# Attention then routed MLP on one core: q of eleven units loaded twice and transposed on VectorE, with their k and v laid nine tokens to a partition

## The chip, the cores and the metric

The kernel runs on one core of one Trainium2 chip. The metric is the device time in microseconds (us) of one execution; several executions are timed and the median is quoted. A separate profile shows one execution of the same program, instruction by instruction. Names used below: PE is the matrix engine (TensorE), ACT is ScalarE, DVE is VectorE, POOL is GpSimd, SP is SyncE, whose queue issues nearly all of the plain DMAs. SBUF is the on-chip memory of 128 partitions, PSUM the accumulators that PE writes.

## The reference

The computation is an attention without a score matrix, followed by a small MLP that only 128 tokens of each batch go through. All data are float32.

```python
# q, k, v: (8 batches, 8 heads, 576 tokens, 64)
q_s = exp(q - max over d) / sum over d            # softmax over the 64 dims
k_s = exp(k - max over tokens) / sum over tokens  # softmax over the 576 tokens
kv  = einsum('bhsd,bhse->bhde', k_s, v)           # 64 x 64 for each head
x   = einsum('bhsd,bhde->bhse', q_s, kv)          # then laid out as (8, 576, 512)
...
scores = x @ w_gate                               # (8, 576)
top = the 128 tokens of the batch with the highest score
out = x; out[top] = x[top] + sigmoid(scores[top]) * (relu(x[top] @ w1) @ w2)
```

w1 is 512 x 1024, w2 is 1024 x 512.

## The kernel before

The attention is cut into 16 units: a unit `u` is four heads of one batch, and two units make a batch. For each unit the kernel loads q, k and v (L115 to L147), takes exponentials on ACT (`k_exp` L266, `q_exp` L271), copies v beside a column of ones (`v_copy` L278), multiplies k by v on PE (`kv_mm` L290), normalises that on DVE (`kv_out` L314), transposes q's exponentials on PE with the identity and copies them from PSUM to SBUF (`q_t` L328), multiplies them by the normalised product (`x_mm` L358), normalises and stores (`x_sums`, `x_scale`, `x_store`, L381 to L408). The softmax sums come out of the same products, through the columns of ones. Inside a unit the heads have the number 2i + a.

Layout. 576 tokens are 64 partitions of nine tokens (T = 9). In units 0 and 1 (`FLAT`, L103) a load puts nine tokens of a head on each of 64 partitions, a = 0 on the lower half of the partitions and a = 1 on the upper half; `kv_mm` then works with 64 x 64 quarters of PE's array (L303 to L306: nine rows by four quarters). In units 2 to 15 k and v are paired: the nine tokens are split five and four over two neighbouring partitions (`R` = 5, `N2` = 4, L138 to L143: two DMAs each for k and v), and `kv_mm` uses all 128 rows (L307 to L311: two banks by five rows by two column halves). q is always nine tokens to a partition and comes in two DMAs of five and four rows (L132 to L137). In `x_mm` every one of the 36 small products takes 64 tokens as stationary operand, `qT[part(i), a, r, c]`, where r and c name the row of the nine.

There are three buffers of q, k and v each (`raw`, LD = 3, L105), so a unit's load has to wait until the exponential three units earlier has read the buffer.

Then for each batch: `score` and `score_row` make the row of scores on all partitions, `compare` counts on DVE for each token how many are higher (L441 to L447, five instructions of 576 elements for a batch), `hits` and `find` turn the ranks into 128 row numbers, `fetch` gathers those rows of the output from DRAM on POOL (L483), `turn` transposes them on PE (L519), `mlp1` and `mlp2` are the two dense products (L535 to L555), and `finish` scatters the result (L563).

Order. The tile scheduler is off (L150); each engine runs its instructions in the order in which they are written, and so does SP's queue of DMAs. The main part is the loop of L746. Step s handles unit s: at its head `find` and `fetch` of an earlier batch when s is even, then `q_t(s)` in two halves (L835, L836), `kv_mm(s + 1)`, `x_mm(s)`, the sums, in odd steps `score` of the batch just completed, then the stores and loads (`queues`, L762: the store of unit s, then k and v of unit s + 3, then its q, the first one held until the last product of `x_mm(s)`), `q_exp(s + 1)`, in odd steps `score_row` and the five `compare`, then `k_exp(s + 2)`, `v_copy(s + 2)` and `hits`. Pieces of the dense products of the batch that is three steps back are spread between these as `pieces(...)`. Steps below 3 are written out above the loop, and step 3 is the branch of L785. In even steps the last pieces are followed by `turn` of the batch whose rows `fetch` has brought.

The x products use two pairs of PSUM banks, which `q_t` uses too; the k by v product and the row of scores share one pair of banks called kv.

Of the kernel before, what the change touches and what calls it, by code (L numbers as in the profile page):

```python
# [17 lines left out]
def kernel(  # L18
# [64 lines left out]
    def pair(tag, bufs=1):  # L83
        return ps.tile([P, 2, 512], F32, tag=tag, name=tag, bufs=bufs)
# [16 lines left out]

    LD = 3
    FLAT = 0, 1  # L103
    RR = 4 * R
    raw = {w: [const.tile([P, 2 * T if w == "q" else RR, D], F32, name=f"{w}{n}") for n in range(LD)] for w in "qkv"}  # L105

    def view(t, paired):
        return t.rearrange("p (h r) d -> p h r d", h=4) if paired else t[:, :2 * T].rearrange("p (i r) d -> p i r d", i=2)
# [6 lines left out]
    def load(u, which, after=None, split=False, flat=False):  # L115
        b, qd = units[u]
        for what in which:
            src = {"q": q, "k": k, "v": v}[what]
            first = src[place(b), 4 * qd].offset
            dmas = []  # L120
            if flat:
                t = view(raw[what][u % LD], False)
                if split:
                    for h, queue in enumerate((nc.scalar, nc.sync)):
                        dmas.append(queue.dma_start(out=t[:, h].rearrange("p r d -> p (r d)"),
                                                    in_=bass.AP(tensor=src.tensor, offset=first + 2 * h * SD,
                                                                ap=[[T * D, P], [1, T * D]])))
                else:
                    dmas.append(nc.sync.dma_start(out=t.rearrange("p i r d -> p i (r d)"),  # L129
                                                  in_=bass.AP(tensor=src.tensor, offset=first,  # L130
                                                              ap=[[T * D, P], [2 * SD, 2], [1, T * D]])))
            elif what == "q":  # L132
                t = view(raw[what][u % LD], False)
                for r0, r1 in ROWS:
                    dmas.append(nc.sync.dma_start(out=t[:, :, r0:r1].rearrange("p i r d -> p i (r d)"),  # L135
                                                  in_=bass.AP(tensor=src.tensor, offset=first + r0 * D,
                                                              ap=[[T * D, P], [2 * SD, 2], [1, (r1 - r0) * D]])))  # L137
            else:  # L138
                t = view(raw[what][u % LD], True)
                for n, rows in ((1, N2), (0, R)):  # L140
                    dmas.append(nc.sync.dma_start(out=t[n::2, :, :rows].rearrange("p h r d -> p h (r d)"),  # L141
                                                  in_=bass.AP(tensor=src.tensor, offset=first + n * R * D,
                                                              ap=[[T * D, 64], [SD, 4], [1, rows * D]])))  # L143
            if after is not None:
                behind(dmas[0], after)
                after = None
        return dmas[-1]  # L147

    ROWS = (0, R), (R, T)
    ctx.enter_context(tc.manual_schedule())  # L150
    load(0, "k", split=True, flat=True)
    load(0, "vq", flat=True)
# [27 lines left out]
    ones_b = const.tile([P, 4 * P], BF16, name="ones_b")  # L180
    nc.vector.memset(ones_b, 1.0)
    w_ps = bank("mm", 2)
    ones_f = const.tile([P, 4 * P], F32, name="ones_f")
    nc.gpsimd.memset(ones_f, 1.0)
    for n in range(WARM):
        nc.tensor.matmul(out=w_ps, lhsT=ones_f[:, :P], rhs=ones_f, start=True, stop=True)
# [20 lines left out]
    for n in range(2):  # L207
        t = const.tile([P, RR, D + 1], F32, name=f"v_ones{n}")
        nc.vector.memset(t[:, :, D:], 1.0)
        v_ones.append(t)  # L210
        t = const.tile([P, 2, C], F32, name=f"kv_w{n}")
        nc.vector.memset(t[:, :, D:D + 1], 1.0)
        kv_w.append(t)
    qrec = const.tile([P, NU, 2, G], F32, name="qrec")
    krec = const.tile([P, NU, 2], F32, name="krec")


    order_minus_p = const.tile([P, RP], F32, name="order_minus_p")
    nc.gpsimd.iota(order_minus_p, pattern=[[1, RP]], base=0, channel_multiplier=-1,
                   allow_small_or_imprecise_dtypes=True)  # L220

# [39 lines left out]
    st = {}  # L261

    def heads(t, u):
        return t[:, :2 * T].rearrange("p (r i) d -> p i r d", i=2) if u in FLAT else view(t, True)

    def k_exp(u):  # L266
        ke = heads(at.tile([P, RR, D], F32, tag="ke", name="ke"), u)
        nc.scalar.activation(out=ke, in_=view(raw["k"][u % LD], u not in FLAT), func=AF.Exp)  # L268
        st["ke", u] = ke

    def q_exp(u, c):  # L271
        if c == 0:
            st["qe", u] = at.tile([P, T, 2, D], F32, tag="qe", name="qe")
        r0, r1 = ROWS[c]
        qr = raw["q"][u % LD].rearrange("p (i r) d -> p r i d", i=2)
        nc.scalar.activation(out=st["qe", u][:, r0:r1], in_=qr[:, r0:r1], func=AF.Exp)  # L276

    def v_copy(u, engine=nc.scalar):  # L278
        out_v, in_v = heads(v_ones[u % 2], u)[:, :, :, :D], view(raw["v"][u % LD], u not in FLAT)
        if engine is nc.scalar:  # L280
            engine.copy(out=out_v, in_=in_v)  # L281
        else:
            engine.tensor_copy(out=out_v, in_=in_v)
# [6 lines left out]
    def kv_mm(u, crossed=False):  # L290

        ke, vo = st.pop(("ke", u)), heads(v_ones[u % 2], u)
        kv_ps = pair("kv")
        if crossed:
            n = 2 * (D + 1)
            for r in range(T):
                for a in range(2):
                    nc.tensor.matmul(out=kv_ps[:, a, :n], lhsT=ke[part(a), :, r],
                                     rhs=vo[part(a), :, r],
                                     start=(r == 0), stop=(r == T - 1))  # L300
            st["kv", u] = [(part(i), kv_ps[part(i), :, i * (D + 1):(i + 1) * (D + 1)]) for i in range(2)]
            return
        for r in range(T if u in FLAT else 0):  # L303
            for i, a in QUARTERS:
                nc.tensor.matmul(out=kv_ps[part(i), a, :D + 1], lhsT=ke[part(a), i, r], rhs=vo[part(a), i, r],
                                 start=(r == 0), stop=(r == T - 1))  # L306
        for a in range(0 if u in FLAT else 2):  # L307
            for r in range(R):
                for i in range(2):
                    nc.tensor.matmul(out=kv_ps[part(i), a, :D + 1], lhsT=ke[:, 2 * i + a, r], rhs=vo[:, 2 * i + a, r],  # L310
                                     start=(r == 0), stop=(r == N2))  # L311
        st["kv", u] = [(slice(0, P), kv_ps[:, :, :D + 1])]

    def kv_out(u):  # L314
# [7 lines left out]
        nc.vector.tensor_mul(prod, kw[:, :, :D], wg[:, qd])  # L322
        nc.vector.reduce_sum(out=kw[:, :, D + 1], in_=prod, axis=AX.X)


    copies = []

# [30 lines left out]
    def x_mm(u, a, wide=False, tag="x"):  # L358

        qT = st["qT", u] if a == 0 else st.pop(("qT", u))  # L360
        x = pair(tag, 2 if tag == "x" else 1)
        kw = kv_w[u % 2]
        for r in range(R):
            for i, c in QUARTERS:
                to = x[part(c), i, r * C:(r + 1) * C]
                if r == N2 and c:
                    last = nc.tensor.matmul(out=to, lhsT=ones_b[part(i), :D], rhs=ones_b[part(i), :C], start=True, stop=True)
                    continue
                if wide and r < N2:
                    if c == 0:  # L370
                        nc.tensor.matmul(out=x[:, i, r * C:(r + 1) * C],
                                         lhsT=qT[part(i), a, r].rearrange("p c t -> p (c t)"), rhs=kw[part(i), a],
                                         start=True, stop=True)
                    continue
                nc.tensor.matmul(out=to, lhsT=qT[part(i), a, r, c], rhs=kw[part(i), a], start=True, stop=True)  # L375
        st["x", u, a] = x[:, :, :R * C].rearrange("p i (r c) -> p i r c", r=R)
        return last

# [113 lines left out]
    def select(b, n, r):  # L492

        k0, m = slots[n]
        if r == 0:
            st["select", n] = bank("mm", 2), md.tile([P, R, P], F32, tag="hit_f", name="hit_f", bufs=1)
        t_ps, hit = st["select", n]
        far = md.tile([P, P], F32, tag="far", name="far")
        nc.scalar.activation(out=far[:, :m], in_=slot_no[:, k0:k0 + m], func=AF.Abs, scale=-1.0,
                             bias=st["rank", b][:, r:r + 1])  # L500
        nc.scalar.activation(out=hit[:, r, :m], in_=far[:, :m], func=AF.Relu, scale=-1.0, bias=1.0)
# [244 lines left out]
    for s in range(LAG, NU + LAG):  # L746
# [83 lines left out]
        else:  # L830
            if chosen is not None and s not in AFTER:
                pieces(1 if here else 2)
                search()
            if here:
                q_t(s, 0)  # L835
                q_t(s, 1, on_vector=s > LAG + 1)  # L836
            if follows:
                kv_mm(s + 1)
                kv_out(s + 1)
# [21 lines left out]
            pieces(0, to=2 if follows else 3)  # L861
            if ends is not None:
                rows()
                ranks()
            if s + 2 < NU:
                k_exp(s + 2)
            pieces(0, to=4)
# [4 lines left out]
                number = count_good(good)  # L872
            if ends is not None:
                each(hits, ends)
            pieces(0, to=KF - 1)
            if second and mlp_b + 1 < B:
                each(turn, mlp_b + 1)
# [35 lines left out]
```

## Time and profile before

| what | value |
|---|---|
| median of 3 timed runs | 209.97 us (209.13 to 210.23) |
| the profiled execution, its own time | 210.15 us |
| its span in the trace | 208.4 us |
| granted clock of PE, mean | 0.988 |
| PE busy | 193.6 us (93%) |
| DVE busy | 119.0 us (57%) |
| ACT busy | 92.1 us (44%) |
| POOL busy | 32.4 us (16%) |
| moved by DMA | 46.66 MB, mean 224 GB/s |

The time of a run stands 1.75 us above the span: the span begins with the first instruction of the core and ends with the last. A busy share is time in which an engine had at least one instruction in it; the chain that ended last, which the profile follows back from the end, tells which of the busy engines the end waited for. The DMA list of the page gives for each kind of load its size and the median time from issue to landing.

### The profile page before, as it was taken

The numbers are of one execution on the slowest core, as the hardware profiler recorded it, in microseconds if no ns is written. First come the engines' busy times: TensorE is split into PE (matmuls) and PEld (weight loads), VectorE is DVE, ScalarE is ACT, GpSimd is POOL, SyncE is SP. The second block draws the span as 40 slices with busy tenths as digits, with TensorE's granted clock in tenths as the row PEclk, the third lists the DMA queues.
The fourth block names the chain that finished last, engine by engine and source line by source line (L and its number), as shares of the span: only waits on it lengthen the run. The fifth ranks groups of instructions, "written<-read, shape, count | busy, mean of one in ns | idle before, by whom it ended". The sixth has DMA issues, their size and how long they took to land.

```text
span 208.4 us, 6943 instructions
## 1 busy us (share of the span) xinstructions
PE 193.6 (93%) x2955; PEld 148.8 (71%) x2955; DVE 119.0 (57%) x361; ACT 92.1 (44%) x135; POOL 32.4 (16%) x93
## 2 busy tenths in 40 slices
PE   7899799798989999999999999999999999999960
PEld 3486789785579848985698759974898579659520
DVE  6668735597167645776378717862776537714010
ACT  3468876574526624545434813672464022111100
POOL 5103000202010101210120104010211012126010
PEclk9999999999999999999999999999999999999995
DMA  6999999999786999995989779895880433131101
GB/s 218 397 307 330 384 360 372 371 381 329 193 296 158 309 327 250 283 279 170 233 282 253 231 175 304 212 314 129 256 247 4 103 110 74 48 101 53 58 5 53
DMA packets 37720, 46.66 MB, mean 224 GB/s; under 512 B 2353, under 2 KB 33073, under 8 KB 37682
## 3 DMA queue, kind: packets, MB, share of 16 engines
q1 hardware_dynamic: 36256, 41.66, 65.2%
q0 software_dynamic: 1280, 4.20, 5.7%
q8 instruction: 25, 0.41, 0.8%
q10 hardware_dynamic: 146, 0.30, 0.5%
q14 instruction: 13, 0.11, 0.2%
HBM read 34.61 MB, written 11.53 MB: 221 GB/s over the span
## 4 chain that ended last, share of the span: by engine, by line
PE 74%; DMA 16%; SPq 3%; issue 1%; ACT 1%; DVE 1%; POOL 0%; POOLq 0%; ACTq 0%
PE mm L544 25%; PE mm L554 25%; DMA k<-in_k_dram 15%; PE x L375 8%; PE kv L310 8%; PE x L349 4%; DMA xr<-out_dram,idx 2%; SPq L141 2%; PE kv L432 2%; PE mm L524 2%; SPq L135 1%; ACT ke L268 1%; PE mm L473 1%; SPq L169 0%; SPq L129 0%
## 5 line engine op out<-in xcount | busy, mean ns | idle before, releaser
L544 PE MATMUL mm<-xT,w 128*128 128x128 f32 x512 | 62.0, 278 | 0.3 <-DVE xT L532 0.3
L544 PEld LDWEIGHTS mm<-xT,w 128*128 128x128 f32 x512 | 58.8, 192 | 2.0 <-ACT xT L532 0.6
L554 PE MATMUL mm<-w,hT 128*128 128x512 f32 x128 | 59.3, 599 | 0.0
L446 DVE SCALAR_TENSOR_TENSOR junk<-srow,s,not_before 128x576 bf16<-128x576 f32 x40 | 32.7, 819 | 9.4 <-ACT srow L438 8.1
L554 PEld LDWEIGHTS mm<-w,hT 128*128 128x128 f32 x128 | 22.6, 190 | 20.6 <-issue 20.1
L567 DVE SCALAR_TENSOR_TENSOR o<-mm,g,xr 128x512 f32<-128x512 f32 x7 | 5.3, 751 | 35.6 <-PE mm L554 35.6
L395 DVE TENSOR_TENSOR xs<-x,qrec 128x640 f32<-128x640 f32 x31 | 24.1, 815 | 0.0
L375 PE MATMUL x<-kv_w,qT 64*64 64x66 f32 x1084 | 21.9, 222 | 1.7 <-issue 1.5
L268 ACT ACTIVATE ke<-k 128x1280 f32<-128x1280 f32 (+1 forms) x16 | 20.0, 1253 | 4.6 <-DMA k<-in_k_dram 4.6
L276 ACT ACTIVATE qe<-q 128x640 f32<-128x640 f32 (+1 forms) x32 | 20.1, 676 | 3.3 <-DMA q<-in_q_dram 3.3
L375 PEld LDWEIGHTS x<-kv_w,qT 64*64 64x64 f32 x1084 | 19.4, 134 | 3.0 <-issue 2.0
L310 PE MATMUL kv<-v_ones,ke 128*64 128x65 f32 x560 | 19.4, 224 | 1.1 <-ACT srow L438 1.1
L310 PEld LDWEIGHTS kv<-v_ones,ke 128*64 128x64 f32 x560 | 17.5, 137 | 2.3 <-ACT srow L438 1.3
L547 ACT ACTIVATE hT<-mm 128x512 f32<-128x512 f32 x16 | 9.6, 597 | 21.5 <-PE mm L544 21.5
L281 ACT COPY v_ones<-v 128x1280 f32<-128x1280 f32 x14 | 17.6, 1257 | 0.7 <-DMA v<-in_v_dram 0.4
L532 ACT COPY xT<-mm 128x512 f32<-128x512 f32 x7 | 4.1, 585 | 30.1 <-PE mm L524 30.1
L487 POOL DMA_INDIRECT xr<-out_dram,idx x8 | 8.3, 1036 | 53.4 <-PE x L349 22.6
L559 POOL DMA_INDIRECT out_dram<-o,idx x7 | 7.0, 996 | 58.9 <-DVE o L567 58.9
L356 ACT COPY qT<-x 128x640 f32<-128x640 f32 (+1 forms) x17 | 11.4, 682 | 9.5 <-PE x L349 8.7
L438 ACT ACTIVATE srow<-kv 128x576 f32<-128x576 f32 x7 | 4.5, 648 | 23.0 <-PE kv L432 23.0
L349 PEld LDWEIGHTS x<-ident,qe 64*128 64x128 f32 x234 | 8.3, 138 | 4.9 <-ACT xT L532 4.5
L354 DVE COPY qT<-x 128x512 f32<-128x512 f32 x11 | 7.6, 692 | 5.8 <-PE x L349 5.8
(115 smaller groups left out, 165.7 us busy)
## 6 DMA issues: line engine op xcount, KB each, us to landing
out_dram<-xs SPq DMA_DIRECT2D x16, 320.0 KB, 3.6
k<-in_k_dram SPq DMA_DIRECT2D x14, 320.0 KB, 5.1
v<-in_v_dram SPq DMA_DIRECT2D x14, 320.0 KB, 6.1
q<-in_q_dram SPq DMA_DIRECT2D x14, 320.0 KB, 6.2
w<-in_moe_w_dram SPq DMA_DIRECT2D x8, 512.0 KB, 7.6
out_dram<-xs SPq DMA_DIRECT2D x16, 256.0 KB, 4.3
k<-in_k_dram SPq DMA_DIRECT2D x14, 256.0 KB, 4.8
v<-in_v_dram SPq DMA_DIRECT2D x14, 256.0 KB, 4.7
```

Of the source, the lines that this page charges most:

```text
L268: nc.scalar.activation(out=ke, in_=view(raw["k"][u % LD], u not in FLAT), func=AF.Exp)
L276: nc.scalar.activation(out=st["qe", u][:, r0:r1], in_=qr[:, r0:r1], func=AF.Exp)
L281: engine.copy(out=out_v, in_=in_v)
L310: nc.tensor.matmul(out=kv_ps[part(i), a, :D + 1], lhsT=ke[:, 2 * i + a, r], rhs=vo[:, 2 * i + a, r], start=(r == 0), stop=(r == N2))
L349: nc.tensor.transpose(out=src[:, a, r], in_=qe[part(a), r0 + r].rearrange("p i d -> p (i d)"), identity=ident[part(a), part(a)])
L356: nc.scalar.copy(out=to, in_=src)
L375: nc.tensor.matmul(out=to, lhsT=qT[part(i), a, r, c], rhs=kw[part(i), a], start=True, stop=True)
L395: nc.vector.tensor_mul(xs[b][:, :, qd, :, a].rearrange("p r i d -> p i r d"), st.pop(("x", u, a))[:, :, :, :D], rec.to_broadcast([P, 2, R, ...
L446: nc.vector.scalar_tensor_tensor(junk, st["srow", b], st["s", b][:, r:r + 1], not_before[:, r], op0=OP.subtract, op1=OP.is_ge, accum_out=s ...
L544: st["piece"] = nc.tensor.matmul(out=h_ps[:, f % 4 * m:(f % 4 + 1) * m], lhsT=w1[:, d, f * P:(f + 1) * P], rhs=xT[:, d, :m], start=(d == 0 ...
L547: nc.scalar.activation(out=hT[:, f - 3:f + 1, :m], in_=h_ps[:, :4 * m].rearrange("p (f c) -> p f c", f=4), func=AF.Relu)
L554: st["piece"] = nc.tensor.matmul(out=st["y", b, n][:m], lhsT=st["hT", b, n][:, f, :m], rhs=w2[:, f], start=(f == 0), stop=(f == KF - 1))
```

## The change

For units 5 to 15 (`TWICE`) three things change.

q's buffers double in size to 4 T rows. q is loaded with four DMAs of 64 partitions, one for each head of the unit. A head's DMA fills 32 partitions with 18 consecutive tokens each, and the next 32 partitions with the same 18 tokens, shifted by 32 elements, so that the upper 32 dims stand where the lower 32 stand in the first copy. A row is 1,120 elements (`ROW`), 4,480 B. ACT takes the exponential of every other run of 32 elements, so that all 64 dims are worked on once.

`q_t` is left out in these units. In its place `q_blocks` transposes 32 x 32 blocks on DVE from SBUF to SBUF, 576 elements a partition in each of two calls, and puts them in token order, which `x_mm` reads through `by_token`. The calls stand one step earlier: the first after `rows()` and ahead of the five `compare`, the second behind `hits` in odd steps and right behind the first in even steps.

k and v of these units use the layout of units 0 and 1: nine tokens to a partition, one DMA each, and the k by v product in quarters of the array. The column of ones of the two v buffers is set again once, on POOL, at units 5 and 6.

Four constants and scratch tiles (`ones_f`, `order_minus_p`, `hit_f`, `far`) move into their upper halves (`spare`), which the units below 5 don't use.

```diff
     LD = 3
     FLAT = 0, 1
+    TWICE = range(5, NU)
     RR = 4 * R
-    raw = {w: [const.tile([P, 2 * T if w == "q" else RR, D], F32, name=f"{w}{n}") for n in range(LD)] for w in "qkv"}
+
+    def level(u):
+        return u in FLAT or u in TWICE
+
+    raw = {w: [const.tile([P, 4 * T if w == "q" else RR, D], F32, name=f"{w}{n}") for n in range(LD)] for w in "qkv"}
+
+    spare = {n: raw["q"][n].rearrange("p r d -> p (r d)")[:, 2 * T * D:] for n in range(LD)}
...
-            if flat:
+            if flat or u in TWICE and what != "q":
                 t = view(raw[what][u % LD], False)
...
+            elif what == "q" and u in TWICE:
+                t = raw[what][u % LD].rearrange("p (a n) d -> p a (n d)", a=2)
+                for a in range(2):
+                    for i in range(2):
+                        dmas.append(nc.sync.dma_start(out=t[part(i), a, :ROW],
+                                                      in_=bass.AP(tensor=src.tensor, offset=first + (2 * i + a) * SD,
+                                                                  ap=[[D // 2, 2], [2 * T * D, 32], [1, ROW]])))
...
     ROWS = (0, R), (R, T)
+    ROW = 2 * T * D - D // 2
...
-    ones_f = const.tile([P, 4 * P], F32, name="ones_f")
+    ones_f = spare[2][:, :4 * P]
...
+    for n in range(LD):
+        nc.gpsimd.memset(spare[n][:, ROW:], 0.0)
...
-    order_minus_p = const.tile([P, RP], F32, name="order_minus_p")
+    order_minus_p = spare[2][:, 4 * P:4 * P + RP]
...
     def q_exp(u, c):
         if c == 0:
             st["qe", u] = at.tile([P, T, 2, D], F32, tag="qe", name="qe")
+        if u in TWICE and u not in FLAT:
+            half = raw["q"][u % LD].rearrange("p (a n) (h s) -> p a n h s", a=2, h=2)[:, c, :, 0]
+            to = st["qe", u].rearrange("p r i d -> p (r i d)").rearrange("p (a n s) -> p a n s", a=2, n=2 * T)
+            nc.scalar.activation(out=to[:, c], in_=half, func=AF.Exp)
+            return
...
+        if u in TWICE[:2]:
+            nc.gpsimd.memset(v_ones[u % 2][:, :2 * T, D:], 1.0)
...
-        for r in range(T if u in FLAT else 0):
+        for r in range(T if level(u) else 0):
             for i, a in QUARTERS:
...
-        for a in range(0 if u in FLAT else 2):
+        for a in range(0 if level(u) else 2):
...
+    def q_blocks(u, a):
+        if u not in TWICE:
+            return
+        if a == 0:
+            st["qT", u] = at.tile([P, 2, R, 2, D], F32, tag="qT", name="qT")
+        to = st["qT", u].rearrange("p a r c d -> p a (r c d)")[:, :, :T * D].rearrange("p a (j t e) -> p a e j t", j=T, e=2)
+        qe = st["qe", u].rearrange("p r i d -> p (r i d)").rearrange("p (a e j s) -> p a e j s", a=2, e=2, j=T)
+        nc.vector.transpose(out=to[:, a], in_=qe[:, a])
...
-                nc.tensor.matmul(out=to, lhsT=qT[part(i), a, r, c], rhs=kw[part(i), a], start=True, stop=True)
+                rows = by_token[part(i), a, R * c + r] if u in TWICE and u not in FLAT else qT[part(i), a, r, c]
+                nc.tensor.matmul(out=to, lhsT=rows, rhs=kw[part(i), a], start=True, stop=True)
...
-            st["select", n] = bank("mm", 2), md.tile([P, R, P], F32, tag="hit_f", name="hit_f", bufs=1)
+            st["select", n] = bank("mm", 2), spare[1][:, :R * P].rearrange("p (r t) -> p r t", r=R)
...
-        far = md.tile([P, P], F32, tag="far", name="far")
+        far = spare[1][:, (R + r % 2) * P:(R + r % 2 + 1) * P]
...
-            if here:
+            if here and s not in TWICE:
                 q_t(s, 0)
-                q_t(s, 1, on_vector=s > LAG + 1)
+                q_t(s, 1)
...
             if ends is not None:
                 rows()
+            if follows:
+                q_blocks(s + 1, 0)
+            if ends is not None:
                 ranks()
+            else:
+                q_blocks(s + 1, 1)
...
             if ends is not None:
                 each(hits, ends)
+                q_blocks(s + 1, 1)
```

## The prediction

> **What bounds the kernel now.** I read four views: the chain that ended last, its pieces in time, the stretches, the groups with the DMA lists.
>
> The page's chain (share of the span by engine, then by line):
>
> ```profile
> PE 74%; DMA 16%; SPq 3%; issue 1%; ACT 1%; DVE 1%; POOL 0%; POOLq 0%; ACTq 0%
> PE mm L544 25%; PE mm L554 25%; DMA k<-in_k_dram 15%; PE x L375 8%; PE kv L310 8%; PE x L349 4%; DMA xr<-out_dram,idx 2%; SPq L141 2%; PE kv L432 2%; PE mm L524 2%; SPq L135 1%; ACT ke L268 1%; PE mm L473 1%; SPq L169 0%; SPq L129 0%
> ```
>
> Its pieces (start, length, what):
>
> ```profile
> 32.04 7.63 DMA k<-in_k_dram
> ...
> 69.58 0.70 PE x L349 x18
> 70.28 1.32 PE kv L310 x40
> 71.60 0.64 PE x L375 x33
> ```
>
> Up to 40 us the end waits for loads; the 7.63 us is mostly queue. From 42 to 180 us the pieces are PE's, but for two gaps of 0.7 and 0.8 us in `x_mm`. Every unit from 4 on has 0.70 us of `q_t` and 1.32 us of `kv_mm` on that path, so PE work removed there is time removed, if nothing else comes late.
>
> Stretches (busy us and instructions of PE, PEld, DVE, ACT, POOL; PE clock; DMA share; GB/s):
>
> ```profile
> 40.00:60.00 20.00, 17.34 (x319) 12.05 (x321) 11.62 (x38) 12.45 (x18) 1.58 (x3) 1.00 0.94 307
> ...
> 103.00:126.00 23.00, 23.00 (x392) 18.17 (x388) 14.45 (x41) 11.55 (x18) 4.07 (x10) 1.00 0.83 244
> ```
>
> PE has no idle time from 103 to 126, and the 16 DMA engines are already at 0.83.
>
> Groups that go, and the DVE row nearest to what comes:
>
> ```profile
> L446 DVE SCALAR_TENSOR_TENSOR junk<-srow,s,not_before 128x576 bf16<-128x576 f32 x40 | 32.7, 819 | 9.4 <-ACT srow L438 8.1
> ...
> L310 PE MATMUL kv<-v_ones,ke 128*64 128x65 f32 x560 | 19.4, 224 | 1.1 <-ACT srow L438 1.1
> ...
> L356 ACT COPY qT<-x 128x640 f32<-128x640 f32 (+1 forms) x17 | 11.4, 682 | 9.5 <-PE x L349 8.7
> ...
> L354 DVE COPY qT<-x 128x512 f32<-128x512 f32 x11 | 7.6, 692 | 5.8 <-PE x L349 5.8
> ```
>
> DMA issues (count, size, median us to landing):
>
> ```profile
> out_dram<-xs SPq DMA_DIRECT2D x16, 320.0 KB, 3.6
> ...
> q<-in_q_dram SPq DMA_DIRECT2D x14, 320.0 KB, 6.2
> ...
> w_row<-in_moe_w_gate_dram ACTq DMA_DIRECT2D x1, 2.0 KB
> ```
>
> The last row has no landing time: that load goes to a single partition, and its semaphore shows two steps instead of 16, one when it is issued and one when data land. All other plain DMAs show sixteen.
>
> [...] Every other plain DMA before has 64 or 128 as its slowest dim, so no run here shows a small dim. [...]
>
> **The change part by part.**
>
> *q's loads.* The source pattern is now [2, 32, 1120]: slowest dim 2, against 64 partitions. [...] each of the unit's four DMAs runs on engines 0 and 1 alone, and each engine carries 32 rows of 4,480 B of each. In the packet records the most frequent times are 46 ns for 1,024 B, 93 for 2,304, 159 for 4,096, 307 for 8,192: a line of 8.4 ns plus 36.7 ns per 1,000 B, so 173 ns for 4,480 B. The second half's rows start 128 B off a 256 B boundary; [...] so I take 178 ns (173 to 195). A unit's q then takes 4 x 32 x 178 = 22.8 us on engine 1, where a step of the loop is 11.1 us (69.58 to 91.86 is two).
>
> Everything else shares those two engines: k and v 32 packets x 93 = 3.0 us a unit, the store 36 x 46 to 72 = 1.7 to 2.6 (2.2), each gather or scatter four packets, 0.7. q of unit 5, issued at 38.8, reaches the engines at about 43.3, behind the queue. From there to the end of q15: 11 x 22.8 = 251, k and v of ten units 30, twelve stores 26, eleven gathers and scatters 7, together 314, so 357 us. The stream has no holes: a unit's load is issued two units ahead, 50 us of work on these engines, and the steps between need less.
>
> What waits: q5 lands at 67 where `q_exp(5)` wants it at 49.3. Behind it ACT has `k_exp(6)`, `v_copy(6)` and the copy of `turn`; DVE has `q_blocks(5)` and what follows. SP's store of unit 3 lies behind q5 in the rings, so `fetch(1)` on POOL and `turn(1)` on PE, at 54.8 before, come after 70. Then every step waits for its q.
>
> At the end, the store of unit 13 lies behind q15 [...], `fetch(6)` takes 1.0 plus 3.3: 365. In the trace of before the chain has `turn(6)` at 167.4, and 41.0 us to the end; less `q_t(15)`, 0.7, that is 40.3: span 405, and with the 1.75 us around it 407. I round to 406.
>
> *PE.* `q_t` of 11 units, 11 x 0.70 = 7.7 us, goes from the path. The quarters: `kv_mm` of unit 0 took 1.28 us for 72 records against 1.32 now, 11 x 0.05 = 0.6. Under the loads above neither is seen, except the 0.7 counted.
>
> *ACT and DVE.* ACT loses 11 copies of 0.69; k_exp and v_copy go from 1.27 to 1.16 us each (rows of L268), q_exp keeps its 1,152 elements. None is on the path. DVE loses 11 copies of 0.69 and gains 22 transposes of 576 elements. [...] I take 0.75, below L446's 0.82, which also accumulates[...]. The first stands where DVE idles 1.07 us before the first `compare` (at 86.24); above 1.07 + 0.2 (`find` follows `hits` by that much) each of five odd steps pays the excess. The others fall into idle time of over 4 us or delay `find`'s sums by 0.2.
>
> *Small edits.* Five POOL memsets of 0.1 to 0.3 us: `order_minus_p`, ready at 2.5, is first read at 4.25, and that gap hides three; the two of v_ones have 6 us before `kv_mm`. The tiles in `spare` are last read at 7.5 and 27 us, before q5 and q7 are written. k and v in one DMA each save two issues, q adds two: nothing.
>
> **Rivals.**
>
> *All 16 engines carry q* (the instruction's pattern is split otherwise than I read it). Then q is 256 x 175 / 16 = 2.8 us a unit in place of 1.7, the engines' work a step is 2.8 + 3.0 + 2.3 + 0.7 = 8.8 of 10.4 us and fits, since landings come 5 us before PE needs them. The gain is 7.7 + 0.6, less 0.5 for `turn(1)`, which already waits for its gather (0.2 us), and 0.5 for PE gaps like the two above: 202.8, against 209.97 of the median 202.7. For it: the trace shows no DMA below 16 engines except one of a single row. It decides from the point where q takes less than 10.4 - 5.9 = 4.5 us a unit on its busiest engine: 16 engines give 2.8, eight 5.7.
>
> *Pairs of engines that differ by partition half.* 11.4 us of q a unit on each: 43.3 + 125 + 63 = 232, and 8 + 40.3 + 1.75 gives 282. [...]
>
> *16 engines, and the gain is eaten.* [...] stores at 72 ns and q at 250 ns fill the engines: about 211. The trace's idle shares speak against it.
>
> **How the numbers follow.** Two engines: 0.85, 406 us, its own range 350 to 450, from a packet at 165 to 195 ns (375 to 430) and from holes in, or relief of, the two engines' stream. 16 engines: 0.10, 202.7. Differing pairs: 0.03, 282. Eaten: 0.02, 211. The range 350 to 450 holds some 0.95 of the first, 0.81 in all. A measurement of this kernel can tell about 0.5% from no change. Faster 0.10; same 0.01; slower 0.89.
>
> **What would show it.** Right: loads of q landing 20 us or more after issue, ACT's `q_exp` waiting for q DMA in all of steps 4 to 14, a mean DMA share far below the 0.83 of before, L349 x36 left, a step of about 28 us between 70 and 350, PE below half busy. Two 576-element transposes a unit near 0.75 us. Wrong: q landing in 5 to 8 us; then the time is near 203 and the chain is PE's throughout.

## The result and the profile after

| | before | after |
|---|---|---|
| median | 209.64 us (209.13 to 210.23, 4 runs) | 403.25 us (401.96 to 404.21, 4 runs) |
| ratio, 95% interval | | 1.923 [1.915, 1.931] |
| profiled execution, span | 210.15 us, 208.4 us | 401.96 us, 400.1 us |
| PE busy | 193.6 us | 211.4 us |
| granted clock of PE, mean | 0.988 | 0.76 |

The changed kernel takes almost twice as long. Where a kernel ran several times, the medians and ratios below are those of its fast runs, which lie within 1.5% of its fastest. The chain that ended last, from its page (by engine, then by line):

```profile
DMA 72%; PE 12%; SPq 10%; ACT 3%; issue 1%; DVE 1%; POOL 0%; POOLq 0%; ACTq 0%
DMA q<-in_q_dram 67%; SPq L143 5%; PE mm L579 4%; DMA out_dram<-xs 3%; PE mm L589 3%; SPq L136 3%; SPq L440 2%; ACT qe L294 2%; DMA xr<-out_dram,idx 2%; PE mm L539 2%; PE x L410 1%; PE x L375 1%; PE mm L559 0%; PE kv L334 0%; ACT ke L285 0%
```

PE had 74% of that chain, and q's loads were not on it. Now they are two thirds of the span (67%). The pieces of the chain in the middle of the run (start, length, what):

```profile
183.57 27.74 DMA q<-in_q_dram
211.31 0.02 issue
211.33 0.02 ACTq L294
211.35 0.04 issue
211.39 0.69 ACT qe L294
212.08 0.09 SPq L143
212.17 0.05 issue
212.22 27.04 DMA q<-in_q_dram
```

The chain is a ring of three: a load of 27 us, the exponential that reads it and frees the buffer, SP's issue of the next load into that buffer. From one load to the next are 28.65 us. The stretches (busy us and instructions of PE, PEld, DVE, ACT, POOL; PE clock; DMA share; GB/s):

```profile
60.00:80.00 20.00, 3.73 (x42) 2.26 (x46) 0.78 (x1) 4.28 (x5) 1.33 (x2) 0.50 0.36 106
...
200.00:228.00 28.00, 16.11 (x208) 11.17 (x207) 10.10 (x28) 5.41 (x8) 0.00 (x0) 0.76 0.38 111
```

The 16 engines together are busy for 0.38 of a step in which everything waits for a DMA, and they move 111 GB/s where the kernel before moved 244 in its loop (103 to 126 us). That fits a load that sits on a few engines. More direct are the packets and the semaphores. Packets of 4,480 B ran in 270 us of the trace: two at a time for 232 us, one for 28, three or four for 10 (from one packet to the next they overlap by 3 to 4 ns). The flat load of one k, queued behind q, shows 14 of its 16 steps between 60.9 and 61.9 us and the last two at 68.67 and 69.87. A q load itself shows three steps, one at its issue and two after. I read a step after the issue as one engine's: two engines carried q, and two were late for k.

The groups (line, engine, operation, count; busy us, mean ns; idle time before, and what ended it):

```profile
L589 PE MATMUL mm<-w,hT 128*128 128x512 f32 x128 | 69.9, 685 | 55.9 <-ACT hT L582 55.9
L559 PE MATMUL mm<-ident,xr 128*128 128x128 f32 x28 | 7.1, 406 | 120.9 <-DMA xr<-out_dram,idx 120.9
...
L294 ACT ACTIVATE qe<-q 128x576 f32<-128x576 f32 x22 | 15.0, 683 | 197.9 <-DMA q<-in_q_dram 197.9
...
L357 DVE STREAM_TRANSPOSE qT<-qe 128x576 f32<-128x576 f32 x22 | 17.1, 775 | 87.4 <-ACT qe L294 87.4
```

ACT stands 197.9 us before the 22 `q_exp`. PE stands 120.9 us before `turn`, because the gathers come behind stores, which lie behind q on the same two engines. The semaphores of the two stores of unit 3 show it: 14 steps of each have come by 57.5 us, the last two at 66.62 and 67.81 for the first store, and at 67.26 and 68.46 for the second; the gather that reads these rows starts at 69.44. L357 is the new transpose, 775 ns.

### The profile page after: what moved, and what is told of

The parts are those of the page before. It is cut to its first block, busy times and chain, and to the rows that moved or that the text cites. A ratio compares the mean times of both kernels' runs of the same rounds, so it can differ in the third digit from the quotient of the medians.

```text
span 400.1 us, 7265 instructions
## 1 busy us (share of the span) xinstructions
PE 211.4 (53%) x3109; PEld 157.2 (39%) x3109; DVE 128.1 (32%) x372; ACT 85.2 (21%) x124; POOL 32.9 (8%) x98
## 4 chain that ended last, share of the span: by engine, by line
DMA 72%; PE 12%; SPq 10%; ACT 3%; issue 1%; DVE 1%; POOL 0%; POOLq 0%; ACTq 0%
DMA q<-in_q_dram 67%; SPq L143 5%; PE mm L579 4%; DMA out_dram<-xs 3%; PE mm L589 3%; SPq L136 3%; SPq L440 2%; ACT qe L294 2%; DMA xr<-out_dram,idx 2%; PE mm L539 2%; PE x L410 1%; PE x L375 1%; PE mm L559 0%; PE kv L334 0%; ACT ke L285 0%
## 5 line engine op out<-in xcount | busy, mean ns | idle before, releaser
L589 PE MATMUL mm<-w,hT 128*128 128x512 f32 x128 | 69.9, 685 | 55.9 <-ACT hT L582 55.9
L559 PE MATMUL mm<-ident,xr 128*128 128x128 f32 x28 | 7.1, 406 | 120.9 <-DMA xr<-out_dram,idx 120.9
L294 ACT ACTIVATE qe<-q 128x576 f32<-128x576 f32 x22 | 15.0, 683 | 197.9 <-DMA q<-in_q_dram 197.9
L559 PEld LDWEIGHTS mm<-ident,xr 128*128 128x128 f32 x28 | 4.7, 206 | 126.5 <-issue 126.5
L357 DVE STREAM_TRANSPOSE qT<-qe 128x576 f32<-128x576 f32 x22 | 17.1, 775 | 87.4 <-ACT qe L294 87.4
L329 PEld LDWEIGHTS kv<-v_ones,ke 64*64 64x64 f32 x936 | 22.4, 191 | 8.1 <-issue 7.9
L329 PE MATMUL kv<-v_ones,ke 64*64 64x65 f32 x936 | 24.5, 280 | 0.0
L285 ACT ACTIVATE ke<-k 128x1152 f32<-128x1152 f32 (+1 forms) x16 | 19.0, 1186 | 23.8 <-DMA k<-in_k_dram 23.8
L410 PEld LDWEIGHTS x<-kv_w,qT 64*64 64x64 f32 x1084 | 22.7, 153 | 1.7 <-ACT ke L285 1.0
L305 ACT COPY v_ones<-v 128x1152 f32<-128x1152 f32 (+1 forms) x14 | 16.6, 1182 | 5.1 <-DMA v<-in_v_dram 5.1
```

Of the source, the lines that this page charges most:

```text
L285: nc.scalar.activation(out=ke, in_=view(raw["k"][u % LD], not level(u)), func=AF.Exp)
L294: nc.scalar.activation(out=to[:, c], in_=half, func=AF.Exp)
L357: nc.vector.transpose(out=to[:, a], in_=qe[:, a])
L410: nc.tensor.matmul(out=to, lhsT=rows, rhs=kw[part(i), a], start=True, stop=True)
L589: st["piece"] = nc.tensor.matmul(out=st["y", b, n][:m], lhsT=st["hT", b, n][:, f, :m], rhs=w2[:, f], start=(f == 0), stop=(f == KF - 1))
```

## The experiments

All runs of before on these chips lie near 212 us (medians 212.40, 211.95, 212.22 and 212.31 in the four groups of runs). Ratios are against those. A row without a ratio is a single timed run. lead_4, lead_8, rows_128, rows_64 and rows_128_crossed load other elements of q, and are for timing alone.

| run | us, median | ratio, 95% |
|---|---|---|
| e_apart | 230.34 | 1.086 [1.078, 1.094] |
| pattern_alone | 283.4 | |
| lead_4 | 286.29 | |
| lead_8 | 236.05 | |
| rows_128 | 219.03 | 1.033 [1.024, 1.042] |
| rows_64 | 224.07 | |
| two_queues | 237.42 | 1.117 [1.108, 1.126] |
| kv_alone | 231.45 | 1.093 [1.087, 1.100] |
| kv_crossed | 216.51 | 1.022 [1.014, 1.030] |
| apart_crossed | 231.56 | 1.090 [1.080, 1.100] |
| rows_128_crossed | 215.69 | 1.016 [1.008, 1.024] |
| late_units | 213.68 | 1.005 [0.999, 1.010] |

### Is it the leading 2 of the pattern?

**e_apart**, the changed kernel with the same 4,480 B rows of q to the same places, but four DMAs by (i, e) in place of (i, a), so that the pattern leads with 32:

```diff
-                for a in range(2):
-                    for i in range(2):
-                        ... out=t[part(i), a, :ROW], ... offset=first + (2 * i + a) * SD,
-                                  ap=[[D // 2, 2], [2 * T * D, 32], [1, ROW]]
+                for i in range(2):
+                    for e in range(2):
+                        p0 = 64 * i + 32 * e
+                        ... out=t[p0:p0 + 32, :, :ROW], ... offset=first + 2 * i * SD + e * (D // 2),
+                                  ap=[[2 * T * D, 32], [SD, 2], [1, ROW]]
```

> The changed kernel with q's four DMAs of a unit cut the other way: one for each half of the partitions and each of the two shifts, both heads in it, so that the slowest dim of the source is 32 and not 2. The same rows of 4,480 B, the same bytes to the same places; nothing else differs. If the slow-down is two engines carrying q [...] all engines carry it: 202.8 us, q landing 5 to 9 us after its issue, the chain PE's from 42 us on. If it is the doubled bytes, the start off a 256 B boundary, the 4,480 B rows or the transposes on DVE, those are all still there and the time stays near 403. If 32 partitions are carried by fewer engines than 16 for another reason, something between, 215 to 290.

230.34 us. The leading 2 accounts for 173 of the 191 us that lie between 403.25 and 212.40, but a second cost of some 18 us stays. A q load shows sixteen semaphore steps here, where it showed two after its issue.

**pattern_alone**, the kernel before, with q of units 5 to 15 in its old amount, in DMAs with a leading 2 (the tokens of q come in another order):

```diff
-   two DMAs of q, ap=[[T * D, P], [2 * SD, 2], [1, rows * D]]
+   four DMAs of q, (i, a), ap=[[T * D, 2], [2 * T * D, 32], [1, T * D]]
```

> The kernel before, with q of units 5 to 15 loaded by four DMAs of 64 partitions whose source pattern has a leading dim of 2 (the even tokens' rows first, then the odd ones'), 2,304 B a row, no byte loaded twice, no transposes on DVE, k and v as before. The tokens of these units stand in another order, so their output rows are permuted. If the leading dim alone decides: 4 x 32 x 93 ns = 11.9 us of q a unit on two engines, 17.4 us a unit with the rest, q15 at about 43 + 131 + 55 = 229 and the end near 279 us. If the slow-down came from the doubled bytes, the misaligned rows or the transposes: 210 us as before.

283.4 us, against 279 expected. Without a byte more of q, without `q_blocks` and with `q_t`, the leading 2 alone costs 71 us. Its chain, from the page:

```profile
DMA 58%; PE 25%; SPq 6%; DVE 4%; issue 3%; ACT 2%; POOL 0%; POOLq 0%; ACTq 0%; DVEq 0%
DMA q<-in_q_dram 31%; DMA out_dram<-xs 23%; PE mm L551 8%; PE mm L561 5%; SPq L136 5%; DMA xr<-out_dram,idx 5%; PE x L382 3%; DVE junk L453 3%; PE mm L511 2%; PE kv L317 2%; ACT qe L283 1%; SPq L412 1%; PE x L356 1%; PE mm L531 1%; PE x L349 1%
```

The stores (`out_dram<-xs`, 23%) are on the chain beside q, as they would be if they wait on the same two engines.

**lead_4** and **lead_8**, the changed kernel with a leading 4 and 8 (other elements of q):

```diff
-   ap=[[D // 2, 2], [2 * T * D, 32], [1, ROW]]
+   ap=[[D // 2, 4], [2 * T * D, 16], [1, ROW]]      lead_4
+   ap=[[D // 2, 8], [2 * T * D,  8], [1, ROW]]      lead_8
```

> The changed kernel with a leading dim of 4 by 16 in place of 2 by 32 in q's source pattern (other elements of q are loaded into the same places, so the values of units 5 to 15 are not those of the reference). [...] 11.4 us of q a unit on each of four engines, 17.3 us with the rest; q15 at about 43 + 125 + 63 = 231 us, the end near 281 us. [...]

> The same with a leading dim of 8 by 8: [...] 5.7 us of q a unit on each of eight engines, 11.6 us with the rest against 10.4 us of PE work a step: the loads set the pace only just, 210 to 225 us. [...]

Had the leading dim not set the number of engines, both were put near 403 or near 203. It is 286.29 us for 4, as expected, and 236.05 for 8, some 11 us above what was expected. The number of engines follows the leading dim in these runs: the semaphore of a q load shows 2, 4 and 8 steps after the one at its issue, and the times are 403, 286 and 236 us. The packets of 4,480 B have a median of 173 ns in all three: at the median they are not slowed, but they are on too few engines. In lead_8 PE waits mostly for gathers before `turn` (total us, times, longest), and this holds with packets of 173 ns; why it is above its expectation was not separated further:

```profile
PE mm L559 <- DMA xr<-out_dram,idx: 22.2, 6, 8.3
```

In e_apart the median of the packets is 319 ns.

### What is the second cost?

**rows_128** and **rows_64** are e_apart with q in two DMAs on all 128 partitions, or four on 64 each (other elements of q, the same number and length of rows):

```diff
-   four DMAs onto 32 partitions, ap=[[2 * T * D, 32], [SD, 2], [1, ROW]]
+   for a: onto t[:, a, :ROW],              ap=[[512, P], [1, ROW]]     rows_128
+   for a, i: onto t[part(i), a, :ROW],     ap=[[512, 64], [1, ROW]]    rows_64
```

> q of units 5 to 15 is loaded in two DMAs onto all 128 partitions, same count of 4,480 B rows as in e_apart, from other elements of q (timing only: the values are not q's own). If the cost left in e_apart (231 us, packets of 319 ns) comes from filling 32 partitions at a time: packets near 173 ns, 200 to 208 us. If it comes from twice the bytes of q: packets stay at 300 ns or more, 225 to 235 us.

> The same with four DMAs onto 64 contiguous partitions each (timing only, other elements of q). [...] packets near 319 ns, 225 to 235 us. [...] packets 160 to 190 ns, 200 to 210 us.

The packets follow the partitions: 173 ns at the median on 128 partitions, 284 on 64, 319 on 32. So 64 came out a little better than 32: below the 319 ns that was put if 64 fill no faster than 32, and far above the 160 to 190 that was put if the rate grows with the partitions. What makes the packets slower on part of the partitions was not shown. rows_128 and rows_64 read the same elements of q, so their difference doesn't come from the source. But the time fell to 219.03 only, where 200 to 208 was expected: neither reading, the partitions or the bytes, named what is left. Waits of PE, in e_apart and then in rows_128, whose profiled execution was the longest of its four runs, 224.43 us (total us, times, longest):

```profile
PE mm L561 <- DMA xr<-out_dram,idx: 10.7, 5, 5.3
PE x L412 <- issue: 5.3, 10, 1.7
PE mm L581 <- issue: 4.1, 3, 2.1
```

```profile
PE x L409 <- issue: 9.6, 13, 3.6
PE mm L578 <- issue: 3.7, 3, 2.1
...
PE mm L558 <- DMA xr<-out_dram,idx: 0.3, 1, 0.3
```

The 10.7 us in which `turn` waited for its gather went with the slow packets; in rows_128_crossed below, a shorter execution of 217.37 us, they are 1.6. What stands is "issue": time in which PE waits for nothing that the profile shows, 13.3 us in these lines against 9.4 in e_apart. rows_64, with slow packets, is 5 us above rows_128, in one timed run; how much of the 11.3 us between e_apart and rows_128 is the packets' rate and how much the order and number of the DMAs was not separated.

**two_queues**, e_apart with the DMAs of partitions 64 to 127 on ACT's queue, to see whether packets get faster when both halves may be written at once:

```diff
-                        dmas.append(nc.sync.dma_start(
+                        dmas.append((nc.sync, nc.scalar)[i].dma_start(
```

> e_apart with the DMAs of partitions 64 to 127 on ACT's queue, so that both halves are written at once. [...] packets between 173 and 250 ns, 203 to 215 us, below before if ACT's four issues a unit cost it nothing. If the bytes are the limit: 231 us as e_apart.

237.42 us, slower than e_apart. The packets have a median of 309 ns on SP's queue and 286 on ACT's, outside the 173 to 250 that was put for halves written at once: the second queue did not bring back the 173 ns of rows_128. Why the run is slower than e_apart is open.

### The other half of the change by itself

**kv_alone**, the kernel before with k and v of units 5 to 15 in the flat layout and `kv_mm` in quarters; q as before:

```diff
+    NINE = range(5, NU)
-            if flat:
+            if flat or u in NINE and what != "q":
-        for r in range(T if u in FLAT else 0):
+        for r in range(T if level(u) else 0):
-        for a in range(0 if u in FLAT else 2):
+        for a in range(0 if level(u) else 2):
```

> Only k and v of units 5 to 15 nine tokens a partition and k by v in quarters, q as before. By the prediction's step: 11 x 0.05 = 0.6 us less, ratio 0.997; a rival: small rows of 64 partitions going makes the loads land sooner before 40 us and gives 1 to 2 us; or more matmuls (72 a unit for 36 or 40) cost 1 us or more.

231.45 us. A part that I had put at a gain of 0.6 us costs 19.5 us. PE's waits:

```profile
PE x L382 <- issue: 10.0, 5, 3.0
PE kv L312 <- issue: 3.5, 9, 0.4
```

One step of its chain (start, length, what):

```profile
79.89 0.70 PE x L356 x17
80.59 0.85 PE kv L312 x46
...
81.50 0.36 PE kv L312 x3
81.86 0.39 issue
82.25 0.53 PE kv L312 x19
...
82.83 0.95 PE x L382 x58
83.79 3.02 issue
86.81 0.27 PE x L382 x2
```

There is no wait for data in this. `kv_mm` goes well until 3 of its matmuls take 0.36 us and PE stands 0.39; `x_mm` goes well until PE stands 3.02 us in the middle of it. The page lists a queue of its own for instructions:

```profile
q8 instruction: 28, 0.46, 0.8%
```

28 packets of 16,384 B. From the trace's records, for each of the five longer gaps of the loop: when it begins, the packet of that queue nearest to it, when PE goes on, and the number of the PE instruction that it goes on with (every record of PE counted in order, those on semaphores too):

```
gap begins   packet on the queue   PE goes on   PE instruction
  47.95       46.95 to  47.92        49.36         1730
  62.83       61.38 to  62.37        63.73         2242
  83.79       84.54 to  85.48        86.81         3010
 124.86      125.22 to 126.24       127.60         4290
 164.52      164.57 to 165.68       167.02         5570
```

The numbers differ by multiples of 256 (2, 3, 5 and 5 times), and PE always goes on 1.33 to 1.44 us after the packet has come. The same border is in the other traces: in rows_128_crossed PE stands 1.30 us before record 1986 and 2.05 before 4290. So PE ran out of instructions at the border of a block, as far as the profile can show it: it names no releaser for these waits. That a block is 256 records of PE and one packet of 16,384 B is an estimate from these numbers; in before the queue has 25 packets beside 5,967 records of PE, one to 239. For 28 packets there are five longer gaps in the loop of kv_alone, of up to 3.02 us, where most of a block lay in the small matmuls: `q_t`, `kv_mm` and `x_mm` follow each other, and the quarters put 144 records of matmuls and weight loads into `kv_mm` where 80 were. The five gaps are 10.6 us together. With nine short ones inside `kv_mm`, 3.5 us, whose cause is open (see the end), and what else differs, PE is idle for 11.5 us more than before. It is also busy for longer, 203.4 us and so 9.8 more, and the two make the span's 21.3. (The timed runs say 19.5; before's trace comes from the runs with a median of 209.64.) The busy time grew for two reasons. The mean clock is 0.965 against 0.988, and the dense products, which the edit does not touch, took 126.7 us where they took 121.3. And k by v itself took 26.1 us in place of 22.0, with the slow matmuls before the short gaps in it.

The sign was in the trace of before. Its two gaps in `x_mm`, 0.69 and 0.83 us, end at PE records 1730 and 1986, which differ by 256, 1.28 and 1.52 us after a packet of 16,384 B. The prediction read these gaps, set 0.5 us aside for more of them in its rival of 16 engines, and did not ask what they were.

**kv_crossed** keeps the flat loads, and replaces the quarters by larger matmuls of which half is not read:

```diff
-        if crossed:
+        if crossed or u in NINE:        # 18 matmuls of 64 x 128 by 130 columns, not 36 of 64 x 64 by 65
```

> kv_alone with the same flat loads, but k by v of units 5 to 15 as 18 matmuls of 64 rows by 128 columns by 130 in place of 72 quarters (the two off-diagonal blocks are computed and not read). Theory: kv_alone's 20 us come from PE running out of instructions, since 144 of kv_mm and 140 of x_mm follow each other and a block of 256 comes late. Then, with 108 instructions a unit fewer, the gaps of 2.5 to 3 us go: 206 to 213 us. Rival: the flat loads of k and v are what costs; then 228 to 234.

216.51 us, 3.5 above the expected range; the profiled execution is the one of 216.51. (A matmul of the code stands in the trace as two: 72 and 36 records, with as many weight loads, so 72 instructions a unit go, not the 108 of the expectation.) What matters is in the waits and the group of `kv_mm`:

```profile
PE x L349 <- issue: 2.0, 1, 2.0
...
PE x L382 <- DVE kv_w L330: 0.2, 1, 0.2
```

```profile
L305 PE MATMUL kv<-v_ones,ke 64*128 64x130 f32 x396 | 24.6, 274 | 0.0
```

No gap of the loop is left, the clock is 0.994, and the same flat loads are in it: the loads were not the cost, the small matmuls were. The run changes their number and their size together, so it does not say by itself which of the two it is; for the five long gaps the borders of the blocks do. `kv_mm` now takes 2.07 us a unit in the chain, against the 1.32 of before, 8.3 us in all, and the span is 6.3 above before's (4.3 by the timed runs).

**apart_crossed** and **rows_128_crossed** make the same edit in e_apart and rows_128.

> e_apart with the same 18 matmuls. [...] the waits for issue (about 13 us over e_apart) go, the waits for gathers behind slow q rows stay, 212 to 222 us. [...] 228 to 234. If instructions alone: 202 to 206.

> rows_128 with the same 18 matmuls (timing only, other elements of q). With neither cost left this is the sum that the rival of 16 engines made: 200 to 206 us. If twice the bytes of q cost PE time by themselves: 215 to 222, as rows_128.

215.69 us for rows_128_crossed: 3.3 less than rows_128, although `kv_mm` costs 8.3 us more PE time than before's. Taking those off gives some 207, an estimate, and the nearest that any run came to a kernel without `q_t`, with neither slow packets nor most of the gaps (3.7 us of "issue" are left in `x_mm`). The run itself, at 1.016 [1.008, 1.024], is no gain and lies at the lower edge of the 215 to 222 that was put for twice the bytes of q costing PE time by themselves. With 8.3 us of larger matmuls in it, it doesn't decide that rival.

apart_crossed is a miss: 231.56 us where 212 to 222 was expected, no less than e_apart, and inside the 228 to 234 that was put for the slow packets alone. `turn` still waits 7.2 us for gathers, and PE stands 3.79 us at one gap without a releaser in `x_mm`. Since the larger matmuls cost 8.3 us of PE time, equal times don't mean that the gaps cost e_apart nothing; the two costs were not separated there.

**late_units**: q twice by e_apart's DMAs in units 13 to 15 alone, where I expected room for DMA, and everything of k, v and k by v as before:

```diff
-    TWICE = range(5, NU)
+    TWICE = range(13, NU)
-            if flat or u in TWICE and what != "q":
+            if flat:
```

> q twice with the 16-engine loads of e_apart for units 13 to 15 alone, whose loads start at 124.7, 135.1 and 146.8 us of before and land 6 to 8 us before they are used; k, v and k by v of all units as before. If the costs are the ones found [...], these loads (5.1 us of all 16 engines a unit at 319 ns a packet, 3.4 more than before) fit, and three q_t of 0.70 us go: 2.1 us less, ratio 0.990. Rival: the late loads hold up a gather or a refill of PE's instructions, and the ratio is 1.00 to 1.02.

213.68 us, ratio 1.005 [0.999, 1.010]: no gain, where 0.990 was expected, and inside the rival's 1.00 to 1.02. The profiled execution (216.92 us, the longest of its runs) has this in its chain:

```profile
139.22 1.34 PE kv L334 x40
140.56 0.14 issue
140.70 10.04 DMA xr<-out_dram,idx
150.73 0.04 issue
150.78 0.71 PE mm L559 x4
```

`turn` waited 2.7 us at 148 for a gather of 10.04 us, while the share of DMA between 130 and 155 is 1.00 to 1.08. In this execution one late gather took more than the 2.1 us that three `q_t` were to give; whether the shorter runs lost it in the same way is not known. No version of this change that I ran is faster than the kernel before.

## Why the prediction was right, and where it was not

**Two engines.** Right in mechanism and size. It was an assumption: before has no plain DMA of fewer than sixteen steps but that of a single row. The changed kernel shows it with two steps and two packets at a time, pattern_alone with 283.4 us, and lead_4 and lead_8 with 4 and 8 steps; the packet records don't say which engines they are. A packet was put at 178 ns: the median is 173, the mean 185. The 5 ns added for rows that start off a 256 B boundary are not seen: half of the rows start so, and 2,135 of the 2,816 packets took just 173 ns. (Two slips in the working change nothing: the most frequent time of 8,192 B before was 309 ns and not 307, which is nearer to the line, and a packet of 165 ns gives 388 us and not 375.) `q_exp`'s second half of unit 5 was to start at 67; ACT's timeline has it and the next two units, with the wait before each in brackets:

```profile
67.09 0.68 ACT L294 ACTIVATE qe<-q 128x576 f32<-128x576 f32 x1 [11.74 <-DMA q<-in_q_dram]
...
95.67 0.68 ACT L294 ACTIVATE qe<-q 128x576 f32<-128x576 f32 x1 [11.79 <-DMA q<-in_q_dram]
...
123.53 0.68 ACT L294 ACTIVATE qe<-q 128x576 f32<-128x576 f32 x1 [11.91 <-DMA q<-in_q_dram]
```

The step is 28 us, as put. **The gather behind q**: `turn(1)` was to come after 70; PE's timeline has

```profile
76.27 1.09 PE L559 MATMUL mm<-ident,xr 128*128 128x128 f32 x4 [20.98 <-DMA xr<-out_dram,idx]
```

**The end.** The last pieces of the chain:

```profile
326.81 25.32 DMA q<-in_q_dram
352.21 0.69 ACT qe L294
...
354.37 3.32 DMA xr<-out_dram,idx
...
357.82 1.09 PE mm L559 x4
```

q15 by 352.2 (357), `turn(6)` at 357.8 (365), from there 42.3 us to the end (40.3). The span is 400.1 for 405: the sum of eleven loads was 5 us too long, since each link is a little shorter (28.5 us against 29.0); from q15 to `turn(6)` were 5.6 us and not 8 (4 of them were put until the store of unit 13 has landed, but the gather's DMA starts 2.16 us after 352.21); and the tail was 2 us too short. PE was to be below half busy: from 70 to 350 us it was, 126.1 of 280 us, but over the whole span, with its start and its end, it was busy for 53%.

**Loads two units ahead** was wrong, without harm. SP stands in the issue itself while so much is queued: four q issues took 13.44 us from 88.72 on, where before's took 0.5 to 0.9 each. So a load runs one link ahead of its use. The stream has no holes all the same.

**PE: the quarters, 0.6 us less.** Wrong in sign. Where nothing stalls, 72 quarters take 1.21 us (at 43.99 in kv_alone) against 1.32, a little better than the 0.05 that I took. But I priced 144 instructions by their time in the array and did not ask how they get to PE. Alone the part costs 19.5 us. Under the loads of the changed kernel it was hidden, where PE stood idle for 20 us at a time, and so the forecast stood; in this part that was luck.

**PE: `q_t` gone, 7.7 us.** PE's work does go, but no run turned it into time: the second copy of q fills the DMA engines (share 1.00 in e_apart from 126 to 150), and gathers waited there (10.7 us before `turn`). The nearest is the estimate of 207 from rows_128_crossed.

**DVE.** 775 ns for a transpose, put at 750. Whether the first one's cover before `compare` holds was not isolated; in the changed kernel DVE waits for q.

**The rivals.** Sixteen engines would have given not 202.8 but about 230 (e_apart): the packets onto 32 partitions are 319 ns and not 175, and the gaps of PE without a releaser (9.4 us in two lines of e_apart's waits) were not in the sum. "It fits" was wrong. My slower version of it, 211, had one half right: it let q's packets slow to 250 ns and fill the engines, and they took 319, with a share of 1.00. It was not the stores (46 ns at the median in e_apart) nor the transposes (775 ns in the changed kernel). Pairs of engines that differ by partition half are out: behind q two of a load's sixteen steps were late and not four, and the time is 403 and not 282.

## What to carry to other kernels

Read the leading dim of a load's source pattern before anything else: with the same number of bytes the kernel took 403, 286, 236 and 230 us with a leading 2, 4, 8 and 32. A load onto 64 partitions was on two engines here, and the mark of it was a mean DMA share of 0.38 in a stretch where everything waits for DMA. When a change splits matmuls into smaller ones, count instructions in a row as well as time in the array: with 64 more a unit the kernel was 19 us slower here, with 10.6 us of gaps at block borders where before had 1.5, and no wait for data to be seen. And ask of every gap that the profile can't explain, however small, what makes it: the two in the trace of before were of the same kind.

## What I had not expected of the hardware

- The profile lists instructions as a DMA queue of their own, 28 packets of 16,384 B in kv_alone. At its five longer gaps, of 0.9 to 3.02 us, the nearest packet took 0.94 to 1.11 us, and PE went on 1.33 to 1.44 us after it had come.
- In the same kernel nine shorter gaps of 0.37 to 0.40 us stand inside `kv_mm`, eight of them right after 3 slow matmuls, and not at borders of blocks. They too are gone in kv_crossed, but e_apart and rows_128 have gaps of the same length in `x_mm`. Their cause is open.
- PE's granted clock was low where PE waited most: in the changed kernel 0.50 from 60 to 80 us, with PE busy for 3.7 of 20 us, 0.76 from 200 to 228, with 16.1 of 28, and 0.93 from 360 to 400, with 32.5 of 40. It is not a function of the busy share alone: in e_apart it was 1.00 from 40 to 60 us, with PE busy for 13.7 of 20. The 128 large matmuls of `mlp2` took 685 ns each in the changed kernel, against 599, which makes 10.6 of the 17.8 us by which PE was busy for longer (211.4 us against 193.6).
- A packet of 4,480 B took 173 ns at the median onto 64 partitions with a leading 2, 4 or 8 (the changed kernel, lead_4, lead_8), 284 onto 64 with a leading 64 (rows_64), 319 onto 32 with a leading 32 (e_apart), and 173 onto all 128 (rows_128). Why was not shown.
